# Softmax attention and an MLP on one core: q of two batches in pair layout, and the first MLP tiles placed ahead of the second attention product

## The chip, the cores and the metric

The kernel runs on one core of a Trainium2 chip. The metric is the device time of one execution in microseconds (us). The core has TensorE (PE) for matrix products, with a second row (PEld) for its weight loads, VectorE (DVE), ScalarE (ACT), GpSimd (POOL) and SyncE (SP), which here does nothing but issue DMAs. SBUF is the working memory with 128 partitions; PE writes its results into PSUM, from which DVE or ACT must move them (an "evacuation").

## The reference

Inputs are q, k and v with 8 batches, 8 heads, 576 tokens and head size 64, and two weight matrices.

```python
q_s = softmax(q, axis=-1)            # over the 64 values of a token
k_s = softmax(k, axis=2)             # over the 576 tokens
kv  = einsum('bhsd,bhse->bhde', k_s, v)
x   = einsum('bhsd,bhde->bhse', q_s, kv)   # then heads side by side: 4608 x 512
h   = x @ w_in                       # 512 -> 2048
out = gelu(h) @ w_out                # 2048 -> 512, float32
```

## The kernel before, in words

The 4608 tokens are worked in nine chunks of 512. Chunk b (0 to 7) holds the first 512 tokens of batch b; the ninth holds the remaining 64 of each batch. All matrix products are bf16.

**Attention of a batch.** q, k and v are loaded as float32 (`load_main` L83, `load_pair` L92). ACT takes the exponential of q (`exp_q` L127) and of k (`exp_k` L147) and writes bf16; v is cast to bf16 with a column of ones beside it (`cast_v` L156), so that one product gives both kv and the sum over tokens that normalises k. `kv_mm` (L188) forms kv for half of the head pairs: 36 matmuls on quarters of the PE array (64 x 64), for two pairs of heads and nine groups of 64 tokens. `kv_norm` (L204) divides on DVE and writes `kvc`. `norm_q` (L228) sums the exponentials of each token on DVE and multiplies by the reciprocal, on POOL or DVE. q must then stand with the head size along the partitions: for batches 0 and 1 `tp_mm` (L243) transposes on PE, eight full 128 x 128 blocks for each half, and `tp_evac` (L261) evacuates into `qT`; later batches use a transposing DMA (`xbar_step` L272). `x_mm` (L284) multiplies `qT` by `kvc`, and `x_evac` (L315) writes `xT`, one tile of 128 x 512 for each head pair.

**MLP of a chunk.** `h_phase` (L335) makes 16 tiles h of 128 x 512, each from four matmuls (dm = 0 to 3, one for each `xT` tile), and ACT applies gelu (L333). `y_phase` makes four tiles of 128 tokens x 512 from 16 matmuls each; they are evacuated to `y_sb` and stored (`y_out` L360).

**Order.** The program writes out the order of every engine by hand (`manual_schedule`); each engine runs its own instructions in that order and waits on semaphores. All loads but the first piece of k go through SP, in the order in which L478 to L499 name them: q, k, v of batch 0, w_in in five blocks, w_out, q and k of batch 1, part of w_out, v of batch 1, and then batch 2. Three tiny loads called `touch` (L485) and that first k piece (L101) go through ACT's queue. A DMA takes one of eight semaphores in turn, so that an issue may first wait until an earlier DMA has landed. PE warms up on zeros (`warm` L472) until data are there.

**Around the change, batch 0** (L506 to L538): exp of q in six instructions and of k in two; norm of q in two halves, POOL and DVE; `tp_mm(0,0)`; two v casts on ACT and two on POOL; `kv_mm(0,0)`, two separate norms; `tp_mm(0,1)`; `x_mm(0,0)`; the first w_in block is cast by ACT (dm = 0) and POOL; `kv_mm(0,1)`, one joint norm; `x_mm(0,1)` (L534); then `h_phase(0)`, whose first group is tiles 0 and 1.

**Batch 1** (L563 to L616) is prepared while PE runs the y tiles of chunk 0: after y step 11 PE does the 16 transposes (L581), after step 13 `kv_mm(1,0)`, after part of step 15 `x_mm(1,0)` and `kv_mm(1,1)`; and two h tiles of chunk 1 are half done ahead of `x_mm(1,1)`. The last four w_out rows (`cast_wo(3, ...)`) arrive and are cast in the same stretch.

Of the kernel before, what the change touches and what calls it, by code (L numbers as in the profile page):

```python
# [16 lines left out]
def kernel(  # L17
# [13 lines left out]

    nc = tc.nc
    B, H, S, D = q.shape
    NT, DM = out.shape
    DF = moe_w_in.shape[1]
    J = 4
# [3 lines left out]
    NDM = DM // 128  # L42
    NDF = DF // 128
    NS = S // 64
    VW = D + 2

    singles = ctx.enter_context(tc.tile_pool(name="singles", bufs=1))
# [35 lines left out]
    def load_main(b, name, t, parts=1):  # L83
# [5 lines left out]
        for i in range(parts):  # L89
            nc.sync.dma_start(out=f[:, i * n:(i + 1) * n, :], in_=src[:, i * n:(i + 1) * n, :])  # L90

    def load_pair(b, name, t, parts=1):  # L92
        f = f32in.tile([128, HP, NS * D], FP32, tag=name + "f")
        st[b][name + "f"] = f
        src = t[b].rearrange("h (p n) d -> (h p) (n d)", n=NS).rearrange("(x q) f -> q x f", q=128)
        n = HP // parts
        for i in range(parts):
            h0 = i * n
            if b == 0 and name == "k" and i == 0:

                nc.scalar.dma_start(out=f[:, 0, :], in_=src[:, 0, :])  # L101
                h0 = 1
            nc.sync.dma_start(out=f[:, h0:(i + 1) * n, :], in_=src[:, h0:(i + 1) * n, :])  # L103
# [20 lines left out]
                in_=q[b, :, M:S, :].rearrange("h p d -> p h d"),  # L124
            )

    def exp_q(b, parts=1):  # L127

        e = attn_sb.tile([128, J, H, D], BF16, tag="eq")
        st[b]["eq"] = e  # L130
        dst = e.rearrange("p j h d -> p h j d")
        src = st[b]["qf"]
        if b == B:
            src = src.rearrange("p j h d -> p h j d")
        else:
            src = src.rearrange("p h (j d) -> p h j d", j=J)
        if parts == 1:
            sets = [(slice(i, None, 4), slice(u, None, 4)) for i, u in ((0, 0), (1, 1), (2, 3), (3, 2))]
        else:
            sets = []  # L140
            for h in (0, 4):
                sets += [(slice(h + i, h + i + n), slice(h + u, h + u + n))
                         for i, u, n in ((0, 0, 2), (2, 3, 1), (3, 2, 1))]
        for i, u in sets:
            nc.scalar.activation(out=dst[:, i], in_=src[:, u], func=AF.Exp)  # L145

# [18 lines left out]
        for hp in range(HP):  # L165
            cast_v(b, hp)

    def kv_tiles(b):


        if b == 0:
            p = [psum_h.tile([128, 512], FP32, tag="h", name="kv")[:, 0:256] for i in range(2)]
            ps = psum_a.tile([128, 4, 256], FP32, tag="a2", name="kv")
            st[b]["kvall"] = ps[:, 0::2]
            p += [ps[:, 0, :], ps[:, 2, :]]
        else:
            ps = psum_a.tile([128, 4, 256], FP32, tag="a2", name="kv")
            st[b]["kvall"] = ps
            p = [ps[:, i, :] for i in place]
        st[b]["kv"] = p  # L180

    place = [1, 2, 0, 3]

# [4 lines left out]
    def kv_mm(b, half):  # L188


        if "kv" not in st[b]:
            kv_tiles(b)
        for n in range(NS):
            for i in range(2):
                for hh in range(2):
                    hp = 2 * half + i
                    pr = slice(hh * 64, hh * 64 + 64)
                    c = slice((hh ^ i) * 64, (hh ^ i) * 64 + 64)
                    nc.tensor.matmul(  # L199
                        st[b]["kv"][hp][c, 0:D + 1], ek[b % 2][pr, hp, n, :],  # L200
                        v_aug[b % 2][pr, hp, n, 0:D + 1], start=(n == 0), stop=(n == NS - 1),
                    )

    def kv_norm(b, half=None):  # L204

        ps = st[b]["kvall"]
        if half is None:
            parts = [(ps, kvc[b], 4)]
        elif b == 0 and half == 0:
            parts = [(st[b]["kv"][hp].unsqueeze(1), kvc[b][:, hp:hp + 1], 1) for hp in range(2)]  # L210
        elif b == 0:
            parts = [(ps, kvc[b][:, 2:4], 2)]
        else:
            parts = [(ps[:, 1:3] if half == 0 else ps[:, 0::3], kvc[b][:, 2 * half:2 * half + 2], 2)]
        for src, dst, m in parts:
            rec = small.tile([128, 4], FP32, tag="reck")
            nc.vector.reciprocal(rec[:, 0:m], src[:, :, D])
            nc.vector.tensor_tensor(  # L218
                out=dst, in0=src[:, :, 0:D],
                in1=rec[:, 0:m].unsqueeze(2).to_broadcast([128, m, D]), op=ALU.mult,  # L220
            )
# [18 lines left out]
            in1=recq.unsqueeze(3).to_broadcast([128, J, w, D]), op=ALU.mult,  # L240
        )

    def tp_mm(b, half):  # L243
        if half == 0:
            st[b]["qT"] = attn_sb.tile([128, J, HP, 128], BF16, tag="qT", name="qT")
        if b == 1 and half == 1:
            ps = psum_a.tile([128, 2, J, 2, 128], BF16, tag="a2", name="tp")[:, 0]
        else:
            pool, tag = (psum_h, "h") if half == 1 else (psum_a, "a")
            ps = pool.tile([128, J, 2, 128], BF16, tag=tag)  # L250
        st[b][f"tp{half}"] = ps
        for i in range(2):
            hp = 2 * half + i
            for j in range(J):
                nc.tensor.transpose(  # L255
                    ps[:, j, i, :],
                    st[b]["eq"][:, j, 2 * hp:2 * hp + 2, :].rearrange("p h d -> p (h d)"),
                    identity,
                )

    def tp_evac(b, half, eng="v"):  # L261
        o = st[b]["qT"][:, :, 2 * half:2 * half + 2, :]
        if eng == "v":
            nc.vector.tensor_copy(out=o, in_=st[b][f"tp{half}"])
        else:
            nc.scalar.copy(out=o, in_=st[b][f"tp{half}"])

    def tp_step(b, half):
        tp_mm(b, half)
        tp_evac(b, half)  # L270

    def xbar_step(b):  # L272
        st[b]["qT"] = attn_sb.tile([128, J, HP, 128], BF16, tag="qT", name="qT")
        nc.sync.dma_start_transpose(
# [9 lines left out]
    def x_mm(b, half):  # L284

        for bb in range(B if b == B else 1):
            for r in range(2):
                for i in range(2):
                    hp = 2 * half + i
                    pr = slice(r * 64, r * 64 + 64)  # L290
                    c = slice((r ^ i) * 64, (r ^ i) * 64 + 64)
                    ps = st[b][f"x{hp}"]
                    if b < B:
                        nc.tensor.matmul(  # L294
                            ps[c, :], kvc_of(b, hp)[pr], st[b]["qT"][pr, :, hp, :],
                            start=True, stop=True,
                        )
                    else:
                        nc.tensor.matmul(  # L299
                            ps[c, bb * R:(bb + 1) * R], kvc_of(bb, hp)[pr],  # L300
                            st[b]["qT"][pr, bb // 2, hp, bb % 2 * R:(bb % 2 + 1) * R],
                            start=True, stop=True,
                        )
# [56 lines left out]
    def y_out(c, ps, j, eng="v"):  # L360
# [2 lines left out]
            nc.vector.tensor_copy(out=y_sb, in_=ps)  # L363
        else:
            nc.scalar.copy(out=y_sb, in_=ps)
        if c < B:
            dst = out[c * S:c * S + M, :].rearrange("(p j) n -> p j n", j=J)[:, j, :]
            nc.sync.dma_start(out=dst, in_=y_sb)
        else:
# [63 lines left out]
    def cast_wi_dm(i, w, dm, eng):  # L433
# [2 lines left out]
        r = n // 128  # L436
        o = wi_bf[:, dm, wi_off[i]:wi_off[i] + n].rearrange("p (c m) -> p c m", c=r)
        w = w[:, dm, 0:n].rearrange("p (m c) -> p c m", c=r)
        if eng is nc.scalar:
            eng.copy(out=o, in_=w)  # L440
        else:
            eng.tensor_copy(out=o, in_=w)

    def load_wo(i):
        w = wst.tile([128, 4, DM], FP32, tag="w")
# [29 lines left out]
            nc.tensor.matmul(ps, z[:, 0:128], z, start=True, stop=True)  # L475


    load_main(0, "q", q, 2)  # L478
    load_pair(0, "k", k, 2)


# [5 lines left out]
    load_pair(0, "v", v, 4)  # L487
    wi = [load_wi(i) for i in range(5)]
    wo = [load_wo(i) for i in range(3)]
    load_main(1, "q", q, 2)  # L490
    load_pair(1, "k", k, 2)
    wo.append(load_wo(3))
    for hp in range(2):
# [10 lines left out]


    table(AF.Exp)  # L506
    exp_q(0, parts=2)
    exp_k(0, parts=2)
    norm_q(0, 0, 2)
    norm_q(0, 1, 2, nc.vector)  # L510
    tp_mm(0, 0)
    cast_v(0, 0, nc.scalar)
    cast_v(0, 1, nc.scalar)
    tp_evac(0, 0, "s")
    warm(1)
    cast_v(0, 2, nc.gpsimd)
    cast_v(0, 3, nc.gpsimd)
    x_tile(0, 0, psum_y, "y")
    x_tile(0, 1, psum_y, "y")
    kv_mm(0, 0)  # L520
    kv_norm(0, 0)
    tp_mm(0, 1)
    tp_evac(0, 1)
    x_tile(0, 2, psum_a, "a")
    x_mm(0, 0)
    x_evac(0, 0, "s")
    cast_wi_dm(0, wi[0], 0, nc.scalar)
    for dm in range(1, NDM):
        cast_wi_dm(0, wi[0], dm, nc.gpsimd)
    kv_mm(0, 1)  # L530
    kv_norm(0, 1)
    x_evac(0, 1)
    x_tile(0, 3, psum_h, "h")
    x_mm(0, 1)  # L534
    x_evac(0, 2, "s")
    x_evac(0, 3)
    cast_wi(1, wi[1], "p")
    table(AF.Gelu)  # L538

    def ybank():  # L540
        return psum_y.tile([128, M], FP32, tag="y", name="ps")
# [3 lines left out]
    def a2bank(i):  # L545
# [2 lines left out]
        return pair[0][:, i]  # L548

    h_phase(0, {  # L550
        0: [lambda: cast_wi(2, wi[2], "v")],
        2: [lambda: cast_wi(3, wi[3], "v")],
        6: [lambda: cast_wi(4, wi[4], "v")],
        9: [lambda: cast_wo(0, wo[0])],
        12: [lambda: cast_wo(1, wo[1])],
    }, groups={0: 2, 4: 4, 8: 4}, banks={
        3: ybank, 6: ybank, 8: ybank,
        9: lambda: psum_a.tile([128, M], FP32, tag="a", name="ps"),
        10: lambda: a2bank(0), 11: lambda: a2bank(1),
    })  # L560


    exp_q(1, parts=2)  # L563
    exp_k(1, parts=2)
    table(AF.Gelu)
    cast_wo(2, wo[2])
    yps = [psum_h.tile([128, DM], FP32, tag="h", name="ps") for j in range(2)]
    yps += [psum_y.tile([128, DM], FP32, tag="y", name="ps") for j in range(2)]
    norm_q(1, 0, 2)
    norm_q(1, 1, 2, nc.vector)  # L570
    cast_wo(3, wo[3], 0, 2)
    for hp in range(HP):
        cast_v(1, hp, nc.gpsimd)
# [4 lines left out]

    for t in range(12):
        y_part(t, range(J))  # L580
    tp_step(1, 0)  # L581
    tp_step(1, 1)
    load(3)
    cast_wo(3, wo[3], 2, 1, "s")
    cast_wo(3, wo[3], 3, 1, "s")
# [36 lines left out]
    h_phase(1, {12: [lambda: cast_v_all(2)]}, t1=4)  # L622


    exp_q(2, parts=2)
    exp_k(2)
    exp_k(3)
    exp_q(3)
# [73 lines left out]
```

The softmax here doesn't subtract the row's maximum and nothing guards it: scores larger than these inputs give would overflow.

## Time and profile before

| what | value |
|---|---|
| median of 3 runs | 279.58 us (279.49 to 279.82) |
| profiled execution, its own time | 279.74 us |
| its span, first to last instruction | 278.0 us |
| PE busy | 270.0 us (97%) |
| ACT, DVE, POOL busy | 158.0, 100.7, 32.8 us |
| DMA | 50.10 MB, mean 180 GB/s |
| first h matmul (L327) begins | 14.3 us |
| batch 0: last piece of q, of k, of v landed | 6.62, 8.96, 11.85 us |
| first w_in block landed | 13.26 us |
| batch 1: last piece of q, of k, of v landed | 33.65, 36.49, 41.94 us |
| full-tile matmul, start to start | 0.215 us |

A row of the profile names a line of the kernel, an engine, an operation and its tiles (out<-in), the number of instructions, their busy time and the idle time of the engine just before them with what ended it. The chain of waits follows the work that ended last back from the end, at each step to what released it. Times count from the start of the span. A matmul's own duration (380 ns) is longer than the step from one to the next, since matmuls are pipelined.

### The profile page before, as it was taken

Reading aid. Unit: us, or ns where it says so; the run is one execution under the profiler, and the core shown is the slowest. Engines: PE = TensorE matmul, PEld = TensorE weight load, DVE = VectorE, ACT = ScalarE, POOL = GpSimd, SP = SyncE. Lnnn points to the kernel's source line nnn. Section 1 sums busy time; section 2 is a strip of 40 time slices with the busy share of each in tenths; the row PEclk is TensorE's granted clock in tenths of the full one; section 3 lists DMA queues with packets and bytes.
Section 4 is the critical chain, followed back from the end, with each engine's and each line's share of the span. In section 5 each row is a group of like instructions: output and inputs, shape, how many; then the busy total and the mean of one; then the engine's idle time right before and its main releaser. Section 6 shows DMA issues by size and latency. Waiting matters only on the chain.

```text
span 278.0 us, 4534 instructions
## 1 busy us (share of the span) xinstructions
PE 270.0 (97%) x1891; PEld 126.5 (46%) x1919; DVE 100.7 (36%) x153; ACT 158.0 (57%) x247; POOL 32.8 (12%) x26
## 2 busy tenths in 40 slices
PE   7899999999999999999999999999999999999995
PEld 3444454444444444444444444444444444444443
DVE  2876574319743540093008400651015200130012
ACT  4867675789377816791569246943683363136400
POOL 1520051002020220014000500050005000000000
PEclk9999999999999999999999999999999999999999
DMA  7999999963993139702981199017502500220033
GB/s 253 398 386 429 397 402 407 398 257 103 287 348 61 66 79 295 283 38 86 267 329 40 42 247 383 38 51 190 115 0 75 151 2 0 75 78 0 0 78 77
DMA packets 44980, 50.10 MB, mean 180 GB/s; under 512 B 20384, under 2 KB 29856, under 8 KB 44704
## 3 DMA queue, kind: packets, MB, share of 16 engines
q1 hardware_dynamic: 44560, 49.39, 53.5%
q10 hardware_dynamic: 400, 0.43, 0.6%
q8 instruction: 15, 0.25, 0.3%
q14 instruction: 5, 0.04, 0.0%
HBM read 36.70 MB, written 9.44 MB: 166 GB/s over the span
## 4 chain that ended last, share of the span: by engine, by line
PE 94%; DMA 2%; issue 1%; ACT 1%; SPq 1%; DVE 0%
PE ps L327 44%; PE ps L355 43%; DMA f<-in_k_dram 2%; PE kv L199 2%; PE ps L294 2%; PE ps L380 1%; PE pair L327 1%; ACT ek L150 0%; ACT v_aug L160 0%; PE ps L255 0%; SPq L90 0%; PE ps L299 0%; SPq L103 0%; PE tp L255 0%; DVE kvc L218 0%
## 5 line engine op out<-in xcount | busy, mean ns | idle before, releaser
L327 PE MATMUL ps<-xT,wi_bf 128*128 128x512 bf16 x557 | 124.2, 380 | 0.5
L355 PE MATMUL ps<-wo_bf,g 128*128 128x512 bf16 x543 | 122.1, 380 | 1.6 <-issue 1.1
L333 ACT ACTIVATE g<-ps 128x512 bf16<-128x512 f32 x142 | 83.5, 598 | 66.8 <-PE ps L327 66.8
L327 PEld LDWEIGHTS <-wi_bf 128*128 128x128 bf16 x576 | 56.1, 98 | 68.0 <-issue 0.5
L355 PEld LDWEIGHTS <-g 128*128 128x128 bf16 x560 | 53.9, 98 | 64.3 <-issue 0.4
L363 DVE COPY y_sb<-ps 128x512 f32<-128x512 f32 x33 | 22.7, 687 | 81.7 <-PE ps L355 78.6
L238 POOL TENSOR_TENSOR e<-e,recq 128x2048 bf16<-128x2048 bf16 (+1 forms) x9 | 25.7, 2855 | 176.2 <-DVE recq L237 141.5
L162 DVE CAST v_aug<-f 128x576 bf16<-128x576 f32 x24 | 16.4, 746 | 47.5 <-DMA f<-in_v_dram 47.5
L236 DVE TENSOR_REDUCE qsum<-e 128x16 f32<-128x1024 bf16 (+1 forms) x13 | 21.1, 1621 | 14.4 <-ACT e L145 14.3
L320 ACT CAST xT<-ps 128x512 bf16<-128x512 f32 x18 | 9.9, 588 | 28.8 <-PE ps L294 18.8
L145 ACT ACTIVATE e<-f 128x512 bf16<-128x512 f32 (+1 forms) x42 | 20.5, 556 | 3.5 <-DMA f<-in_q_dram 3.5
L150 ACT ACTIVATE ek<-f 128x2304 bf16<-128x2304 f32 (+1 forms) x10 | 17.2, 1728 | 0.5 <-DMA f<-in_k_dram 0.4
L318 DVE CAST xT<-ps 128x512 bf16<-128x512 f32 x17 | 11.0, 686 | 17.0 <-PE ps L294 14.1
L79 ACT ACT_TABLE_LOAD x9 | 11.5, 1283 | 2.8 <-issue 2.6
L475 PE MATMUL ps<-zeros 128*128 128x512 f32 (+1 forms) x15 | 9.2, 773 | 1.5 <-DVE zeros L500 1.5
L145 ACT ACT_TABLE_LOAD x7 | 9.0, 1283 | 0.1
L431 DVE CAST wi_bf<-w 128x512 bf16<-128x512 f32 x12 | 7.3, 654 | 2.2 <-DMA w<-in_moe_w_in_dram 1.9
L199 PEld LDWEIGHTS <-ek 64*64 64x64 bf16 x576 | 6.6, 105 | 2.6 <-ACT wo_bf L470 0.4
L199 PE MATMUL kv<-v_aug,ek 64*64 64x65 bf16 x576 | 7.2, 194 | 0.2 <-ACT v_aug L160 0.2
L294 PE MATMUL ps<-qT,kvc 64*64 64x512 bf16 x62 | 5.7, 391 | 0.8 <-DVE kvc L218 0.6
L238 DVE TENSOR_TENSOR e<-e,recq 128x1024 bf16<-128x1024 bf16 x4 | 6.2, 1546 | 0.1
L475 PEld LDWEIGHTS ps<-zeros 128*128 128x128 f32 x14 | 3.5, 260 | 6.0 <-issue 4.5
(39 smaller groups left out, 49.9 us busy)
## 6 DMA issues: line engine op xcount, KB each, us to landing
out_dram<-y_sb SPq DMA_DIRECT2D x32, 256.0 KB, 2.4
f<-in_k_dram SPq DMA_DIRECT2D x6, 1152.0 KB, 9.7
f<-in_v_dram SPq DMA_DIRECT2D x6, 1152.0 KB, 11.7
f<-in_q_dram SPq DMA_DIRECT2D x6, 1024.0 KB, 7.2
w<-in_moe_w_in_dram SPq DMA_DIRECT2D x6, 512.0 KB, 8.7
f<-in_v_dram SPq DMA_DIRECT2D x8, 288.0 KB, 6.8
f<-in_q_dram SPq DMA_DIRECT2D x4, 512.0 KB, 12.5
w<-in_moe_w_out_dram SPq DMA_DIRECT2D x2, 1024.0 KB, 11.7
```

The source lines that it names most:

```text
L79: nc.scalar.activation(out=scr[:, 1:2], in_=scr[:, 0:1], func=func)
L145: nc.scalar.activation(out=dst[:, i], in_=src[:, u], func=AF.Exp)
L150: nc.scalar.activation(out=ek[b % 2][:, i:i + n], in_=st[b]["kf"][:, i:i + n].rearrange("p x (n d) -> p x n d", n=NS), func=AF.Exp,)
L162: eng.tensor_copy(out=o, in_=i)
L199: nc.tensor.matmul(st[b]["kv"][hp][c, 0:D + 1], ek[b % 2][pr, hp, n, :], v_aug[b % 2][pr, hp, n, 0:D + 1], start=(n == 0), stop=(n == NS - 1),
L236: nc.vector.reduce_sum(out=qsum, in_=eq[:, :, hs, :], axis=AX.X)
L238: eng.tensor_tensor(out=eq[:, :, hs, :], in0=eq[:, :, hs, :], in1=recq.unsqueeze(3).to_broadcast([128, J, w, D]), op=ALU.mult,)
L327: nc.tensor.matmul(ps, wi_bf[:, dm, t * 128:(t + 1) * 128], st[c]["xT"][:, dm, :], start=(dm == 0), stop=(dm == NDM - 1),)
L333: nc.scalar.activation(out=st[c]["g"][:, t, :], in_=ps, func=AF.Gelu)
L355: nc.tensor.matmul(ps, st[c]["g"][:, t, j * 128:(j + 1) * 128], wo_bf[:, t, :], start=(t == 0), stop=(t == NDF - 1),)
L363: nc.vector.tensor_copy(out=y_sb, in_=ps)
L475: nc.tensor.matmul(ps, z[:, 0:128], z, start=True, stop=True)
```

## The change

Two things are changed together.

**Order in batch 0.** Tiles 0 and 1 of h are begun (dm = 0 and 1) ahead of `x_mm(0,1)` and ended (dm = 2 and 3) after it. `kv_mm(0,0)` gets the two-bank PSUM tile and one joint norm; `kv_mm(0,1)` gets two banks of the h pool and two norms. ACT evacuates xT tiles 0, 1 and 3 and DVE tile 2 (before: ACT 0 and 2, DVE 1 and 3). All four casts of the first w_in block are POOL's.

**q of batches 0 and 1.** A head pair has one head in partitions 0 to 63 and the other in 64 to 127, with eight consecutive tokens of 64 values in each partition (before: four tokens of all eight heads in each of 128 partitions). So q comes in four DMAs of 64 partitions (pieces of 2 KB) in place of two of 128 partitions (pieces of 1 KB). Exp is two instructions in place of six. The transposes are quarters of the array, 32 for each half in place of eight full ones, and the evacuations are four of 128 x 512 in place of two of 128 x 1024. The tokens of an output tile then lie in two interleaved sets of 64 rows, so that each of the chunks' y tiles is stored with two DMAs of 64 partitions.

```diff
+    def load_qpair(b):
+        f = f32in.tile([128, HP, M], FP32, tag="qf", name="f")
+        st[b]["qf"] = f
+        src = q[b, :, 0:M, :].rearrange("(x q) (p n) d -> q p x (n d)", q=2, n=NQ)
+        for i in range(2):
+            for hh in range(2):
+                nc.sync.dma_start(
+                    out=f[hh * 64:hh * 64 + 64, 2 * i:2 * i + 2, :], in_=src[hh, :, 2 * i:2 * i + 2, :]
+                )
...
+    def exp_qpair(b):
+        e = attn_sb.tile([128, HP, NQ, D], BF16, tag="eq", name="e")
...
+    def norm_qpair(b, i, eng):
+        eq = st[b]["eq"][:, 2 * i:2 * i + 2].rearrange("p x n d -> p (x n) d")
...
+    def tpq_mm(b, half):
+        if half == 0:
+            st[b]["qT"] = attn_sb.tile([128, HP, NQ, 64], BF16, tag="qT", name="qT")
+            tp = [psum_a.tile([128, 2, NQ, 64], BF16, tag="a", name="tp")]
...
+        for n in range(NQ):
+            for i in range(2):
+                for hh in range(2):
+                    pr = slice(hh * 64, hh * 64 + 64)
+                    c = slice((hh ^ i) * 64, (hh ^ i) * 64 + 64)
+                    nc.tensor.transpose(
+                        st[b]["tp"][i][c, half, n, :], st[b]["eq"][pr, 2 * half + i, n, :],
+                        identity[pr, pr],
+                    )
...
+        if c < 2:
+            dst = out[c * S:c * S + M, :].rearrange("(p j i) n -> j i p n", j=J, i=2)
+            for i in range(2):
+                nc.sync.dma_start(out=dst[j, i], in_=y_sb[i * 64:i * 64 + 64, :])
...
-    load_main(0, "q", q, 2)
+    load_qpair(0)
...
-    load_main(1, "q", q, 2)
+    load_qpair(1)
...
-    exp_q(0, parts=2)
+    exp_qpair(0)
     exp_k(0, parts=2)
-    norm_q(0, 0, 2)
-    norm_q(0, 1, 2, nc.vector)
-    tp_mm(0, 0)
+    norm_qpair(0, 0, nc.gpsimd)
+    norm_qpair(0, 1, nc.vector)
+    tpq_mm(0, 0)
     cast_v(0, 0, nc.scalar)
     cast_v(0, 1, nc.scalar)
-    tp_evac(0, 0, "s")
+    tpq_evac(0, 0, "s")
+    tpq_evac(0, 1, "s")
...
     kv_mm(0, 0)
     kv_norm(0, 0)
-    tp_mm(0, 1)
-    tp_evac(0, 1)
-    x_tile(0, 2, psum_a, "a")
+    tpq_mm(0, 1)
+    tpq_evac(0, 2)
+    tpq_evac(0, 3)
     x_mm(0, 0)
     x_evac(0, 0, "s")
-    cast_wi_dm(0, wi[0], 0, nc.scalar)
-    for dm in range(1, NDM):
+    x_evac(0, 1, "s")
+    for dm in range(NDM):
         cast_wi_dm(0, wi[0], dm, nc.gpsimd)
     kv_mm(0, 1)
     kv_norm(0, 1)
-    x_evac(0, 1)
+    h_begin(0)
+    hps = [psum_h.tile([128, M], FP32, tag="h", name="ps"),
+           psum_a.tile([128, 2, M], FP32, tag="a2", name="ps")[:, 0]]
+    for dm in (0, 1):
+        for t in range(2):
+            h_mm(0, hps[t], t, (dm,))
     x_tile(0, 3, psum_h, "h")
     x_mm(0, 1)
-    x_evac(0, 2, "s")
-    x_evac(0, 3)
+    x_evac(0, 2)
+    x_evac(0, 3, "s")
     cast_wi(1, wi[1], "p")
     table(AF.Gelu)
+    for dm in (2, 3):
+        for t in range(2):
+            h_mm(0, hps[t], t, (dm,))
+    for t in range(2):
+        h_gelu(0, hps[t], t)
+    cast_wi(2, wi[2], "v")
...
-    exp_q(1, parts=2)
+    exp_qpair(1)
...
-    tp_step(1, 0)
-    tp_step(1, 1)
+    tpq_mm(1, 0)
+    tpq_evac(1, 0)
+    tpq_evac(1, 1)
+    tpq_mm(1, 1)
+    tpq_evac(1, 2)
+    tpq_evac(1, 3)
```

## The prediction

> **What bounds the kernel now.** I read the page's parts 1 and 2, then the chain of waits, then the DMA view.
>
> ```profile
> PE 270.0 (97%) x1891; PEld 126.5 (46%) x1919; DVE 100.7 (36%) x153; ACT 158.0 (57%) x247; POOL 32.8 (12%) x26
> ```
>
> TensorE is busy almost throughout, so time can only be won or lost where it starts late or stalls. The chain, in order of time (start, us, what), shows that start:
>
> ```profile
> 2.34 6.62 DMA f<-in_k_dram
> 8.98 1.16 ACT ek L150
> 10.15 1.15 ACT v_aug L160 x2
> 11.33 0.47 PE kv L199 x34
> 11.81 0.55 PE ps L255 x8
> 12.36 0.52 PE ps L294 x2
> 12.88 0.53 PE kv L199 x31
> 13.43 0.18 DVE rec L217
> 13.64 0.30 DVE kvc L218
> 13.98 0.41 PE ps L294 x4
> 14.39 0.75 PE ps L327 x3
> ```
>
> The reader should see a load as the first 9 us: the last part of k is queued behind all of q. The PE work before 10 us is warm-up. After it, PE waits once more, 13.4 to 13.98, for batch 0's second kv normalisation. From 14.3 us the MLP streams at 0.215 us a matmul, and 15.20 is where dm = 2 of tiles 0 and 1 begins.
>
> The stages next (length; busy time of PE, PEld, DVE, ACT, POOL; clock, DMA share, GB/s):
>
> ```profile
> 14.30:28.10 13.80, 13.70 (x66) 6.25 (x65) 9.43 (x15) 9.83 (x18) 1.36 (x3) 1.00 1.04 410
> 28.10:38.50 10.40, 10.35 (x48) 4.70 (x48) 7.31 (x8) 7.50 (x11) 1.90 (x1) 1.00 1.04 400
> 38.50:45.50 7.00, 6.80 (x116) 3.66 (x117) 4.29 (x10) 3.48 (x7) 2.70 (x4) 1.00 1.06 402
> ```
>
> The DMA engines are full up to 45.5 us. So a load that takes more engine time delays everything queued behind it, up to batch 1's v. How near that v is to being late stands in the timeline:
>
> ```profile
> 41.29 1.37 POOL L162 CAST v_aug<-f 128x576 bf16<-128x576 f32 x2 [1.34 <-DMA f<-in_v_dram]
> 43.27 0.51 PE L199 MATMUL kv<-v_aug,ek 64*64 64x65 bf16 x36
> ```
>
> POOL waits for v, ends the casts at 42.66, and PE uses them at 43.27: 0.6 us of slack.
>
> Last, the DMA view of two stretches: 268.2 to 271.5 us, where two stores of 64 partitions lie alone, and 11.5 to 13.5 us, with 1 KB packets into all 128 partitions (packets, MB, share of 16 engines).
>
> ```profile
> q1 hardware_dynamic: 160, 0.26, 34.1%
> out_dram<-y_sb SPq DMA_DIRECT2D x2, 128.0 KB, 2.2
> ```
> ```profile
> q1 hardware_dynamic: 772, 0.77, 108.9%
> ```
>
> First: 0.341 x 3.3 us x 16 / 128 data packets = 141 ns for a 2 KB packet (the packet records give a mean of 137, median 146; 32 of the 160 packets are semaphores). Second: 1.089 x 2 x 16 / 772 = 45 ns for 1 KB (records: 46). A 2 KB packet of a 128-partition load takes 84 in the records. A 64-partition transfer thus runs at some 60% of the full rate.
>
> [...] no load of 2 KB pieces into 64 partitions is in this trace. [...] The trace shows 36 quarter matmuls in 0.41 us (41.29 to 41.70).
>
> **The change, part by part.** Sums are made against the profiled execution: 279.74 us, of which 278.0 is span and 1.74 around it; the median of the runs is 0.16 lower.
>
> *q loads.* Two DMAs of 512 KB (1024 packets of 1 KB) become four of 256 KB (512 packets of 2 KB), each into 64 partitions. Before: 1024 x 46 / 16 = 2.9 us of full engines. After: 512 x 137 / 16 = 4.4. Ends: 512 x 84 / 16 = 2.7 if alternate halves overlapped, a gain of 0.25; 512 x 147 / 16 = 4.7 without any overlap. I take **+1.5 us per load**, as the stores are the nearest row. It happens twice (batches 0 and 1), with DMA full behind both.
>
> *What the two extra issues move.* An issue takes SP some 0.5 us. More important, eight DMAs may be outstanding, each on its own semaphore, and by the waits in the changed build SP's first k issue waits for the k part that ACT loads (landed 3.88), its second for the first q part, and the v issues behind it for the tiny touch loads (5.2, 6.5). So k is issued at about 3.9 instead of 1.8. A quiet store has its first packet 0.83 us after issue, so k is ready at 4.8, while q streams until about 2.3 + 0.8 + 4.4 = 7.5: hidden. If q were fast (until 5.8) it would still be hidden.
>
> *Exp and norm of q, batch 0.* One 128x1024 exp for three: about 1.05 us (128x1152 takes 1.16) for 1.24. ACT then waits for k anyway, so nothing. Both norms stay as they are.
>
> *Quarter transposes.* 32 for 8 in each half: at the kv pace, 32 x 0.41/36 = 0.36 us against 0.45 now[...]. From −0.1 to +0.45 each, four times, two of them on PE's path in batch 1. I take 0.
>
> *Evacuations.* ACT gets two of 128x512 (0.58 each by the xT row) for one of 1.00. They end at 1.16 after the v casts; kv_mm and its norm (0.5 + 0.5) cover nearly all: +0.05.
>
> *Batch 0 in sequence,* with +1.5 on each landing. v part 1: 10.46 to 11.96; k's last: 8.96 to 10.46. ACT: exp k to 11.62, casts to 12.9. kv_mm 12.9, kvc at 13.9 (one joint norm for two), x_mm 14.05, both evacuations now on ACT: xT0 15.1, xT1 15.7. The first w_in block lands 13.26 + 1.5 = 14.8; all four casts, one of which ACT did before, go to POOL at 0.37 each: 15.2, 15.55, 15.9, 16.3. So the h matmuls that now stand ahead of the second x run from 15.2 and 15.75 to 16.2. kv_norm 1 (two parts, 0.8 for 0.5) is ready at 15.5 and hidden. But x_mm 1 follows only at 16.2, and its evacuation (0.45 to its start, 0.7 long) has **nothing left to hide it**: dm = 2 begins at 17.4, where it was 15.2. So +2.2: 1.5 from the load, 0.7 from the order. The 0.6 us wait for kvc goes; the wait for the last two xT takes its place.
>
> *Batch 1.* By then the DMA queue is 2 x 1.5 = 3.0 late and PE 2.2. The norm of q's second half ends near 41.1 (landing 33.65 + 3.0, exp 1.05, sum 1.2, reciprocal 0.25, product 1.6 with gaps), behind it on DVE the w_out cast to 41.75; y tile 12, due at 39.40 + 2.2 = 41.6, waits 0.15. v's last: lands 41.94 + 3.0 = 44.95, cast to 45.7; kv_mm is then due at 43.27 + 2.35 = 45.6. So PE is late by 3.0 − 0.6 = **2.4**.
>
> *Stores.* Batches 0 and 1 store 64 rows at a time: 8 issues more on SP, 0.4 us each, and 128 packets a tile at 137 ns for 84, so 0.4 us more of the DMA engines for each of eight tiles. Behind them stand the loads of batches 3 and 4 and the transposing DMA of batches 2 and 3; those loads are used over 5 us after landing. Nothing.
>
> Sum: span 278.0 + 2.4 = 280.4; with 1.74 around it 282.1, on the median **282.0 us**.
>
> **Rivals.**
> - *The halves overlap* (the other side). Place: the q loads. If packets into alternate halves run at 84 ns, each load wins 0.25 and only the order's 0.7 is lost, with x evacuation partly covered: about +0.3, so 279.9, not slower by what can be told. It decides from a mean packet of 92 ns downwards (2.94 x 16 / 512). For it: four DMAs queue together, not two. Against: the stores. If besides the wait for xT is less than reckoned, this case ends faster, near 279.0.
> - *The queue runs dry.* v's issues wait for the touch loads; if these land past 9.5 us, v comes later than its place in the queue by 1 us or so: 283.0. Against: q's slow stream covers them.
> - *Quarters don't run in parallel,* so the change's array use is not what it says: 2 x 0.45 more on PE in batch 1: 282.9. Against: the kv row.
>
> **How the numbers follow.** Likeliest 0.74; halves overlap 0.14 (within 0.2%: 0.09, faster 0.05); queue dry 0.06; quarters serial 0.06. A measurement of this kernel can tell about 0.2%, 0.56 us. The likeliest's own range is 281.2 (load +1.1) to 283.0 (load +1.8); the whole range, 280.2 to 283.3, takes in the dear cases and half-overlapping loads and leaves out the overlap case. Faster 0.05, same 0.09, slower 0.86.
>
> **What would show it.** q packets of 2 KB near 137 ns, and k's last landing near 10.5 us; first kv_mm at 12.9; after x_mm 1 a PE gap of about 0.8 us for xT; batch 1's last v landing near 45; from there a constant shift. Wrong: q packets near 84, or a kv_mm start before 11.6.

## The result, and the profile after

The changed kernel takes 287.34 us (median of six; 284.92 to 287.75) against 279.53 before; the ratio of the means is 1.0267 (1.0232 to 1.0301). It is slower, as forecast, but by 7.8 us and not 2.4, and outside the range. The profiled execution is the fastest of the six (284.92 us); the five others lie between 287.18 and 287.75, and run 11 gives a profile of such a usual execution. All ratios in this document are of fast executions; the only slow one in all runs is one of run 10, at 285.22 us.

The page's busy row and the row of the granted TensorE clock, in 40 slices of 7.1 us:

```profile
PE 271.7 (96%) x1987; PEld 127.1 (45%) x2015; DVE 99.6 (35%) x155; ACT 157.1 (55%) x238; POOL 33.8 (12%) x27
PEclk9979999999999999999999999999999999999999
```

The "7" is what no step of the prediction had: for one stretch of 3.4 us, 14.29 to 17.71, TensorE had half its clock. Before, the clock never fell while TensorE worked (1.00 from 6.70 us to the end of the span). (The row shows 9 for the start too, but there the record of the clock has nothing: it begins at 6.70 us before and 7.46 after, and up to then the warm-up matmuls step 0.85 us, from then on 0.43. All stretches below are falls after that.)

The chain of waits up to 20 us (start, us, what):

```profile
2.21 5.45 DMA f<-in_q_dram
7.67 7.37 DMA w<-in_moe_w_in_dram
15.10 1.49 POOL wi_bf L466 x4
16.64 1.06 PE ps L350 x2
17.70 0.41 PE ps L318 x4
18.12 0.68 DVE xT L341
18.80 1.58 DVE wi_bf L458 x3
```

This is the predicted sequence: q's DMAs hold the queue, the first w_in block lands late (15.04), POOL casts it alone, the h matmuls run ahead of x (L318), and x's evacuation (xT) stands in the open. But it runs on to 18.8 (18.12 + 0.68; the last row is DVE's next cast) where 17.4 was foreseen. Of the DMA view, 32.5 to 35 us, q of batch 1:

```profile
DMA packets 362, 0.69 MB, mean 275 GB/s; under 512 B 38, under 2 KB 38, under 8 KB 362
q1 hardware_dynamic: 362, 0.69, 107.0%
```

1.07 x 2.5 us x 16 engines / 324 data packets = 132 ns for a packet of 2 KB in this stretch: near the 137 taken from the stores (over the whole load the packet records give a mean of 122). Batch 1 in the timeline, first before, then after:

```profile
38.51 0.61 PE L255 MATMUL ps<-identity,e 128*128 128x128 bf16 x8
38.95 0.61 PE L255 MATMUL tp<-identity,e 128*128 128x128 bf16 x8
```
```profile
42.25 0.45 PE L177 MATMUL tp<-identity,e 64*64 64x64 bf16 x32
43.22 0.77 PE L177 MATMUL tp<-identity,e 64*64 64x64 bf16 x32 [0.53 <-DVE qT L185]
43.98 1.37 POOL L218 CAST v_aug<-f 128x576 bf16<-128x576 f32 x2 [0.67 <-DMA f<-in_v_dram]
45.75 0.48 PE L251 MATMUL kv<-v_aug,ek 64*64 64x65 bf16 x36
```

The second half of the quarter transposes waits 0.53 us for DVE to evacuate the first half's first PSUM tile, and some 0.3 more for the second one, inside the row (0.77 us where the first half took 0.45): both halves share two PSUM tiles now, where each half of the full blocks had one of its own. The prediction had no such wait. v is cast at 45.35, and kv follows without a wait.

To compare runs, five marks on TensorE: Y0 and Y1, the first y matmul of chunks 0 and 1; H1 and H2, the first h matmul of chunks 1 and 2; Y8, the first y matmul of the last chunk. Before they stand at 28.15, 58.42, 44.16, 74.34 and 260.56 us. Shifts against that, in us, one profiled execution each, with the stretches of half clock after the warm-up and before the last matmul:

```
run                     Y0     H1     H2     Y8    half clock (us)
after                 +3.65  +4.53  +4.97  +4.96   14.3-17.7
1  order only         +0.53  +0.53  +0.53  +0.52   none
2  q only             +5.08  +6.16  +6.61  +6.60   14.9-21.8
3  after, warm 6      +2.22  +7.20  +7.73  +7.73   44.9-48.3
4  after, q 128       +0.44  +1.32  +1.80  +1.79   none
5  before, 4x64       +2.50  +7.45  +7.46  +7.45   11.6-15.0, 45.7-49.2
6  before, 4x128      +1.48  +1.48  +1.49  +1.48   none
7  q 128, edits       +0.38  +1.18  +1.18  +1.18   none
8  after, edits       +4.38  +4.95  +4.96  +4.95   11.5-18.4
9  4x64, batch 1      -0.31  +5.89  +5.90  +5.90   40.8-47.6
10 4x128, touch k     +4.66  +4.66  +4.67  +4.67   14.9-21.7
11 after again        +6.03  +6.91  +7.33  +7.32   12.9-23.1
12 best of q 128      -0.08  +0.37  +0.37  +0.37   none
13 4x128, no touch    +0.68  +1.23  +2.15  +2.13   none
14 before, 2x64       +6.65  +7.25  +7.26  +7.25   12.3-22.6
```

From H2 on every run keeps its shift: what moves TensorE happens before H2, in the first 75 to 82 us.

### The profile page after: what moved, and what is told of

Read it like the earlier page. It is cut to its first block, busy times and chain, and to the rows that moved or that the text cites. A ratio compares the mean times of both kernels' runs of the same rounds, so it can differ in the third digit from the quotient of the medians.

```text
span 283.1 us, 4742 instructions
## 1 busy us (share of the span) xinstructions
PE 271.7 (96%) x1987; PEld 127.1 (45%) x2015; DVE 99.6 (35%) x155; ACT 157.1 (55%) x238; POOL 33.8 (12%) x27
## 4 chain that ended last, share of the span: by engine, by line
PE 76%; DMA 14%; DVE 5%; ACT 2%; issue 1%; SPq 1%; POOL 1%; ACTq 0%
PE ps L350 36%; PE ps L378 35%; DMA f<-in_q_dram 6%; DMA out_dram<-y_sb 3%; DMA w<-in_moe_w_in_dram 3%; PE ps L318 2%; PE kv L251 1%; DMA qT<-e 1%; PE ps L407 1%; DVE qsum L288 1%; DVE qsum L155 1%; DVE wi_bf L458 1%; SPq L101 1%; DVE e L157 1%; ACT e L201 1%
## 5 line engine op out<-in xcount | busy, mean ns | idle before, releaser
L290 POOL TENSOR_TENSOR e<-e,recq 128x2048 bf16<-128x2048 bf16 (+1 forms) x7 | 21.9, 3129 | 152.5 <-DVE recq L289 124.9
L288 DVE TENSOR_REDUCE qsum<-e 128x32 f32<-128x2048 bf16 (+1 forms) x9 | 16.2, 1802 | 10.9 <-ACT e L201 10.9
L341 DVE CAST xT<-ps 128x512 bf16<-128x512 f32 x16 | 10.4, 686 | 18.1 <-PE ps L318 15.3
L201 ACT ACTIVATE e<-f 128x512 bf16<-128x512 f32 x28 | 15.3, 617 | 0.1
L155 DVE TENSOR_REDUCE qsum<-e 128x16 f32<-128x1024 bf16 x4 | 4.8, 1205 | 9.3 <-ACT e L144 9.3
L157 POOL TENSOR_TENSOR e<-e,recq 128x1024 bf16<-128x1024 bf16 x2 | 3.8, 1902 | 29.0 <-DVE recq L156 29.0
L458 DVE CAST wi_bf<-w 128x512 bf16<-128x512 f32 x12 | 6.6, 620 | 0.2
L492 DVE CAST wo_bf<-w 128x2048 bf16<-128x2048 f32 (+1 forms) x4 | 4.8, 1206 | 4.9 <-DMA w<-in_moe_w_out_dram 4.9
```

Of the source, the lines that this page charges most:

```text
L288: nc.vector.reduce_sum(out=qsum, in_=eq[:, :, hs, :], axis=AX.X)
L290: eng.tensor_tensor(out=eq[:, :, hs, :], in0=eq[:, :, hs, :], in1=recq.unsqueeze(3).to_broadcast([128, J, w, D]), op=ALU.mult,)
L341: nc.vector.tensor_copy(out=st[b]["xT"][:, hp, :], in_=ps)
```

## The experiments

**1 and 2: each part alone.** Run 1 has the new order with the old q; run 2 the new q with the old order.

```diff
# 1: after, with load_main / exp_q / norm_q / tp_mm / tp_evac of before for q
# 2: after, with the order, casts, PSUM tiles and evacuations of batch 0 of before
```

> The order alone: q of batches 0 and 1 is loaded, transposed and stored as in the kernel before; in batch 0 the first h matmuls stand ahead of the second x product, with the kv tiles, norms, evacuations and casts of the changed kernel. The theory that the order costs 0.7 us (the evacuation of the last two xT tiles has no cover left): 279.6 + 0.3 to 0.8 = 280.0 to 280.4, clock 1.00. The rival that the order is what gives TensorE its gaps and so halves its clock: a window at half clock, 281.5 or more.

> The q part alone (loads into 64 partitions, quarter transposes, stores of 64 rows, and exp of batch 2 in four instructions), in batch 0 with the order of the kernel before. The theory that the load is the cost and the clock only follows from gaps that the order makes: 279.6 + 1.8 (start) + 0.9 (batch 1) + 0.4 (batch 2) = 282.5 to 283, clock 1.00. The rival that the late load itself leaves TensorE too idle in one window, whatever the order: half clock appears here too, 284.5 to 287.5.

Measured: order alone 1.0025 (1.0015 to 1.0034), 280.3 us; q alone 1.0254 (1.0234 to 1.0273), 286.8 us. The order's timeline on TensorE:

```profile
13.57 1.04 PE L385 MATMUL ps<-xT,wi_bf 128*128 128x512 bf16 x3 [0.48 <-DVE kvc L276]
14.53 0.41 PE L353 MATMUL ps<-qT,kvc 64*64 64x512 bf16 x4
15.73 1.45 PE L385 MATMUL ps<-xT,wi_bf 128*128 128x512 bf16 x6 [0.79 <-POOL wi_bf L486]
```

h starts earlier (14.32 before), but x ends at 14.9 and dm = 2 begins only 0.8 us later, at 15.73 instead of 15.20: +0.53, where +0.7 was foreseen. The row names a cast of POOL for this wait; the last two xT evacuations end at the same moment, at 15.61 and 15.68. Nearly all of the loss is the q part, and run 2 loses its clock too, with the old order: its rival came true.

**3: does the clock make the rest?** More warm-up matmuls ahead of the first kv, so that TensorE isn't idle there.

```diff
-    warm(1)
+    warm(6)
     cast_v(0, 2, ...)
```

> The changed kernel with six instead of one warm-up matmul between the first transposes and kv_mm of batch 0, which fills the idle time of TensorE there. The theory that the half clock costs 1.4 us in the profiled execution and 4 in the usual one: clock 1.00 and 282.8 to 283.8. The rival that the clock matters little and the loads set the time: 286.5 to 287.5 as the changed kernel.

Measured: 1.0353 (1.0333 to 1.0373), 289.2 us: slower than the change itself. The expectation that the filler gains in total fell, but it splits the loss in two. At the start the clock did not fall; there dm = 2 began at 17.42, for the 17.4 foreseen, and Y0 is +2.22 us, for +2.2:

```profile
17.42 6.63 PE L350 MATMUL ps<-xT,wi_bf 128*128 128x512 bf16 x30 [0.79 <-POOL wi_bf L455]
```

The half clock moved into batch 1:

```profile
41.75 0.45 PE L177 MATMUL tp<-identity,e 64*64 64x64 bf16 x32 [0.86 <-POOL e L157]
44.23 0.77 PE L177 MATMUL tp<-identity,e 64*64 64x64 bf16 x32 [2.04 <-DVE qT L185]
45.34 3.15 PE L378 MATMUL ps<-wo_bf,g 128*128 128x512 bf16 x7 [0.33 <-issue]
48.42 0.48 PE L251 MATMUL kv<-v_aug,ek 64*64 64x65 bf16 x36
```

TensorE now comes to batch 1 only 2.2 us late, finds q not normalised (0.86), then waits 2.04 for the evacuation, which stands on DVE behind the w_out cast; then seven matmuls take 3.15 us, 0.45 each, twice the full-clock step. In this execution the last q of batch 1 landed at 38.01, later than in the changed kernel's first profile (36.75). There a late q of batch 1 is hidden because the start is later still.

**4 and 7: the same layout from 128 partitions.** Partition p of a head takes tokens 9p to 9p + 7, so that two heads of 64 partitions are one DMA of 128 with the same 2 KB pieces (token 9p + 8 goes to the ninth chunk). Run 7 adds y step 11 between the two transpose halves, evacuates the first half on ACT, and takes the exp of batch 2's q in six instructions again. The change had made them four (`exp_q(2)`), a part of it that neither its description nor the prediction has.

```diff
-        src = q[b, :, 0:M, :].rearrange("(x q) (p n) d -> q p x (n d)", ...)
-            for hh in range(2):
-                nc.sync.dma_start(out=f[hh*64:hh*64+64, 2*i:2*i+2, :], in_=src[hh, ...])
+        src = q[b].rearrange("h (p n) d -> (h p) (n d)", n=9).rearrange("(x q) f -> q x f", q=128)
+            nc.sync.dma_start(out=f[:, 2*i:2*i+2, :], in_=src[:, 2*i:2*i+2, 0:M])
```

> The changed kernel, but batches 0 and 1 keep tokens 9p to 9p+7 in partition p and leave tokens 9p+8 to the last chunk, so that a q load is two DMAs of all 128 partitions in pieces of 2 KB; all else is unchanged, stores too. The theory that 64 partitions make the load slow: v of batch 0 lands 0.2 us earlier than in the kernel before (10.2 to 10.5 us), no half clock, and 279.6 + 0.7 (order) + 0.4 (exp of batch 2) = 280.3 to 281.3. The rival that two more issues and their waits for semaphores delay the queue[...]: the same, as the issues go too; then the mean packet of q in the changed kernel tells them apart, and here 84 ns a packet is expected. The rival that neither is the cause: 285 to 287.5.

> The run with q loads of 128 partitions, with two edits more: in batch 1 one y step stands between the two halves of the transposes, and ACT evacuates the first half (so the second half no longer stands waiting for that evacuation, whose PSUM tiles it shares); and the exp of batch 2 is again six instructions, so that the first half's norm need not wait for the second. The theory that these two waits are the 0.9 us (batch 1) and 0.5 us (batch 2) that the stage times of that run show beyond the kernel before: 281.1 to 281.6, with the stages as long as before within 0.2 us. The rival that quarter transposes themselves are slower: batch 1 keeps 0.5 us or more, 282 or more.

Measured: run 4 1.0112 (1.0096 to 1.0127), 282.7 us, of which the marks show 1.8; its profile ends 4.6 us after the last matmul, for 3.4 before, which is most of the rest; run 7 1.0063 (1.0045 to 1.0081), 281.5 us. The DMA view of 3 to 9 us, first the changed kernel, then run 4:

```profile
DMA packets 969, 1.68 MB, mean 280 GB/s; under 512 B 184, under 2 KB 184, under 8 KB 969
```
```profile
DMA packets 1295, 2.42 MB, mean 404 GB/s; under 512 B 191, under 2 KB 191, under 8 KB 1295
```

With 128 partitions the queue is back at full rate (q packets 84 to 86 ns), k's last part lands at 8.65 and not 10.84, no stretch of half clock is left while TensorE works, and Y0 is +0.44. So the load carries the start's loss, the clock's share included. Run 4 also has two DMAs less for each q; runs 5, 6, 13 and 14 tell that from the 64 partitions. What stays, +0.88 from Y0 to H1 and +0.48 from H1 to H2, is not the load: it is the same +0.88 and about the same +0.44 as in the changed kernel. Run 7 takes the second away wholly (Y1 to H2 15.93 us as before, for 16.40); the first stayed at 0.80, where the expectation was 0.2 at most: ACT got to the evacuation only at 39.09, behind an ACT table load, and the second transposes still waited for it.

**5, 9 and 14: the slow load alone.** The kernel before, with q in halves of the partitions: run 5 in four DMAs in both batches, run 9 in batch 1 only, run 14 in two DMAs (no extra issue).

```diff
-            nc.sync.dma_start(out=f[:, i*n:(i+1)*n, :], in_=src[:, i*n:(i+1)*n, :])
+            for u in range(0, 128, 64):          # 14: all eight heads in each half
+                nc.sync.dma_start(out=f[u:u+64, i*n:(i+1)*n, :], in_=src[u:u+64, ...])
```

> The kernel before, with only the q loads of batches 0 and 1 cut into four DMAs of 64 partitions (pieces of 1 KB as before), layout and all else unchanged. The theory that loading half of the partitions is what costs: the DMA rate falls to 200 to 300 GB/s while q lands, v of batch 0 lands 1.5 to 2 us later, and with the idle time of TensorE a window at half clock: 283 to 287. The rival that the quarter transposes and their waits are the larger part: 280 to 282.

> The kernel before, with only batch 1's q loaded in four DMAs of 64 partitions; batch 0 is untouched. The theory that such a load slows the queue for 6 us (to 200 to 290 GB/s) and that v of batch 1 has 0.6 us of slack: start as before, y of chunk 0 to the next h 2 to 3 us longer, or 4 to 5 with a window at half clock: 281.7 to 284.7. The rival that batch 1 was late in the runs with both loads only because it inherited batch 0's delay: 279.6 to 280.5.

> The kernel before with q of batches 0 and 1 in two DMAs, each of 64 partitions and all eight heads, in place of two of 128 partitions and four heads; as many issues, k issued as early as before. The theory that 64 partitions slow the queue by themselves: the DMA rate is 200 to 300 GB/s while q lands, k's last part lands 1 us or more later than 8.96, and batch 1's v 2 us or more later than 41.9; 283 to 287. The rival that only the number of issues counts: landings within 0.4 us of the kernel before, and 279.6 to 281 (exp of q's first half must now wait for all of q).

Measured: run 5 1.0227 (1.0194 to 1.0260), run 9 1.0198 (1.0152 to 1.0244), run 14 1.0290 (1.0259 to 1.0321). Run 5, the kernel before with nothing but the load changed, loses 6.1 us, for the change's 7.8; less of it falls at the start (Y0 +2.50) and more in batch 1, where nothing hides the late q. Run 14 loses 7.8, but there each DMA brings all eight heads, so that the exp of q can't begin before all of q has landed (9.15 us); TensorE stands idle for 4.40 us before its first transposes, at 14.13. In run 14 the DMA view of 3 to 9 us has, where it had 386 GB/s before:

```profile
DMA packets 1360, 1.56 MB, mean 259 GB/s; under 512 B 143, under 2 KB 1119, under 8 KB 1360
```

k's last part lands at 11.21 in run 14, with two DMAs, and at 11.22 in run 5, with four: two suffice, so their number isn't the cause. Run 9 shows batch 1 without the start's delay as cover; its timeline, of ACT, POOL and TensorE:

```profile
35.00 1.28 ACT L147 ACT_TABLE_LOAD   x1 [6.37 <-DMA f<-in_q_dram]
39.23 1.90 POOL L240 TENSOR_TENSOR e<-e,recq 128x1024 bf16<-128x1024 bf16 x1 [23.75 <-DVE recq L239]
41.18 1.03 PE L257 MATMUL ps<-identity,e 128*128 128x128 bf16 x8 [2.82 <-POOL e L240]
43.33 3.58 PE L357 MATMUL ps<-wo_bf,g 128*128 128x512 bf16 x8
```

q comes late (its last part lands at 37.09, for 33.65 before), its exp and norm with it, TensorE idles 2.82 us, and then runs at half clock (eight transposes 1.03 us for 0.61, eight matmuls 3.58 for 1.89). One execution of run 9 kept the full clock: 283.27 us, against 285.66 to 286.46. By that one execution a slow q in batch 1 costs 3.6 us by its wait (283.27 − 279.72) and 2.4 to 3.2 more by the clock, if it isn't hidden. Runs 9 and 14 came out above their expected ranges (281.7 to 284.7, 283 to 287), by the clock in run 9.

**6, 10 and 13: the extra issues alone.** q in four DMAs of 128 partitions. In run 6 SP's k issues wait for semaphores (1.3 us), as in the changed kernel; run 10 adds a tiny early load on k (in place of that on w_out), in case untouched memory was slow; run 13 leaves the three tiny loads out, so that semaphores are free.

```diff
-    load_main(0, "q", q, 2)        # and batch 1
+    load_main(0, "q", q, 4)
# 10: the third touch reads k instead of w_out;  13: no touch
```

> The kernel before, with only the q loads of batches 0 and 1 cut into four DMAs of two heads each, over all 128 partitions: as many issues and the same waits for semaphores as in the changed kernel. The theory that the number of issues is hidden: 279.4 to 280.1. The rival that the issues and their semaphores delay k and v: 281 or more.

> The run with q in four DMAs over all partitions, with one edit: the third tiny early load reads 16 rows of k of batch 0 in place of w_out. In that run k and v packets of up to 1.4 us stood at 6.8 to 9 us, where the kernel before has none over 0.33. The theory that k's first accesses are slow when they come late and nothing has touched that memory before: with k touched those packets are gone, k's last part lands at 9.0 us in place of 10.4, and 279.6 to 280.4. The rival that the place of the issues in the queue does it: as that run, 281 to 284.5.

> The kernel before with q of batches 0 and 1 in four DMAs over all partitions, and without the three tiny early loads, so that eight DMAs suffice for q, k and the first v piece and k is issued without waiting for a semaphore. The theory that the wait for a semaphore (k issued at 4 us, behind which its packets come in with gaps) is the 1.4 us: k's last part lands at 9.0 to 9.3 in place of 10.4 to 10.7. The rival that the number of DMAs itself disturbs the queue: still 10.4 or later. What v and the weights lose without their early touch comes on top, after that.

Measured: 1.0105 (1.0051 to 1.0160), 1.0120 (1.0086 to 1.0154) and 1.0069 (1.0040 to 1.0097). SP's issues in run 6 and in run 13:

```profile
0.73 2.01 SPq L90 DMA_DIRECT2D f<-in_q_dram  x4
4.07 0.82 SPq L103 DMA_DIRECT2D f<-in_k_dram  x2
```
```profile
0.73 1.99 SPq L90 DMA_DIRECT2D f<-in_q_dram  x4
2.77 0.95 SPq L103 DMA_DIRECT2D f<-in_k_dram  x2
```

Issued at 4.07, k's last part lands at 10.44; at 2.77, at 9.63, between what the theory and the rival of run 13 had; before (1.79), at 8.96. In run 6, 17 packets of k and v (2304 bytes each) took over 300 ns after 6.5 us, up to 1449; in run 13 none did. Run 10 has them too (18), so untouched memory isn't the reason; what makes them long stays open. Run 13 also loses 0.9 us between Y1 and H2, which was not followed up. Behind a slow q this wait is hidden: run 5 has it and run 14 hasn't, and their k lands at 11.22 and 11.21.

Run 10 prices the clock. Its executions fall into two groups: four at 280.6 to 281.4 us (mean 281.0) with a mean clock of 0.998 or more, seven at 283.8 to 284.6 (mean 284.2) with 0.988, which is two stretches. The same program with two stretches of half clock takes 3.2 us more. The first group has no profile, so its loads may have landed earlier as well; run 6, profiled without a stretch, has k 0.29 us earlier than run 10 (10.44 for 10.73) and Y8 3.19 us earlier, which leaves some 2.9 for the clock.

**8 and 11: the changed kernel again.** Run 8 has run 7's two edits on it; run 11 is the change once more, for a second profile.

```diff
-    exp_q(2)
+    exp_q(2, parts=2)
...
-    tpq_evac(1, 0); tpq_evac(1, 1)
+    tpq_evac(1, 0, "s"); tpq_evac(1, 1, "s"); y_part(11, range(J))
```

> The changed kernel with those same two edits, q loads of 64 partitions kept. The theory that the loads make the start and the waits make much of batch 1's loss: the stage of batch 1 (y of chunk 0) takes 16.0 to 16.5 us where the changed kernel's took 16.9, and 284.5 to 286 in all. The rival that batch 1 simply waits for the late loads: the stage as long as in the changed kernel and 286.5 to 287.3.

> The changed kernel once more, for a second profiled execution, since the first was the fastest of six, with one window at half clock where the others have a mean clock that fits two or three. Theory: the usual execution also has a window at half clock in batch 1 (42 to 50 us), where TensorE waits for q and its transposes; the median stays at 287.3. Rival: it is the start that has more windows.

Measured: run 8 1.0236 (1.0182 to 1.0291), 285.4 us; run 11 1.0255 (1.0235 to 1.0275), 286.9 us. Run 8's Y0 to H1 is 16.58 us, for 16.89 in the changed kernel and 16.01 before: a part of that wait is gone. Its H1 to H2 is 30.19 us, for 30.62 in the changed kernel and 30.18 before. The wait behind this second one: first SP and TensorE of the changed kernel, then of run 8:

```profile
72.15 1.69 SPq L297 DMA_TRANSPOSE qT<-e  x1
75.94 0.63 PE L318 MATMUL ps<-qT,kvc 64*64 64x512 bf16 x8 [0.37 <-DMA qT<-e]
```
```profile
71.64 1.83 SPq L303 DMA_TRANSPOSE qT<-e  x1
75.93 0.63 PE L324 MATMUL ps<-qT,kvc 64*64 64x512 bf16 x8
```

The transposing DMA needs the exp and norm of q; with four coarse instructions instead of six it starts later, and x of batch 2 waits 0.4.

Run 11 is a usual execution of the change: three stretches of half clock, all at the start and none in batch 1, as the rival had it. TensorE there:

```profile
11.04 0.44 PE L177 MATMUL tp<-identity,e 64*64 64x64 bf16 x32 [1.05 <-POOL e L157]
11.41 0.39 PE L499 MATMUL ps<-zeros 128*128 128x512 bf16 x1
12.95 0.26 PE L251 MATMUL kv<-v_aug,ek 64*64 64x65 bf16 x2 [1.14 <-ACT v_aug L216]
13.52 0.70 PE L251 MATMUL kv<-v_aug,ek 64*64 64x65 bf16 x34 [0.31 <-ACT v_aug L216]
```

q and v are late, the warm-up has run out, and TensorE works for a moment and waits for another. The busy times of whole clock windows show what follows (from:to and length; busy time and instructions of PE, PEld, DVE, ACT, POOL; granted clock, DMA share, GB/s). First run 11:

```profile
9.46:12.87 3.41, 1.30 (x35) 0.53 (x34) 2.56 (x3) 2.58 (x4) 1.52 (x1) 1.00 1.04 401
12.87:16.28 3.41, 2.65 (x109) 2.13 (x109) 1.42 (x6) 2.29 (x6) 2.17 (x5) 0.50 1.08 396
16.28:19.70 3.42, 2.63 (x9) 0.67 (x9) 1.51 (x5) 1.32 (x3) 1.79 (x4) 0.50 1.05 400
```

then the changed kernel's profiled execution:

```profile
10.88:14.29 3.41, 1.79 (x84) 1.21 (x88) 2.17 (x5) 3.25 (x6) 1.51 (x3) 1.00 1.06 395
14.29:17.71 3.42, 3.04 (x77) 1.64 (x74) 1.45 (x6) 1.07 (x2) 2.78 (x7) 0.50 1.07 402
```

and the kernel before, at its weakest:

```profile
10.11:13.52 3.41, 3.05 (x94) 2.08 (x92) 2.25 (x7) 2.50 (x5) 1.54 (x3) 1.00 1.07 391
```

Here the windows of 3.41 us in which TensorE was busy for 1.30 (38%) and 1.79 (52%) were followed by one at half clock; the one with 3.05 (89%) wasn't. At half clock, the windows with 2.65 and 2.63 (78%, 77%) were followed by half clock again, the one with 3.04 (89%) by full clock.

**12: a version that loses nothing?** The 128-partition q in the old order, both first halves evacuated on DVE with y step 11 between, and batch 2's exp in six.

> q loads of 128 partitions in two DMAs (tokens 9p to 9p+7), order of batch 0 as in the kernel before, exp of batch 2 in six instructions, and the transposes' second halves not held up: the first halves are evacuated on DVE, and in batch 1 a y step stands between. Theory: every known cost is out; the load is some 0.3 us shorter and the start is as before or 0.2 earlier; stages of batch 1 and 2 as before: 279.3 to 279.9, no clear difference. Rival that quarter transposes or the stores of 64 rows cost by themselves: 280.3 or more.

Measured: 1.0038 (1.0025 to 1.0050), 280.7 us, clock full, Y0 −0.08. That is above the expected range and in the rival's, but the trace shows one more wait. H1 keeps +0.37; the second transposes take 0.77 us again:

```profile
39.06 0.77 PE L185 MATMUL tp<-identity,e 64*64 64x64 bf16 x32
```

Two of them start at 39.06, the others from 39.39 on, when DVE has evacuated the first half's second tile, behind a w_out cast. So the quarter transposes cost by this wait and not by their own pace. This version still doesn't gain over the kernel before, and the profile (280.22 us, the fastest of its six) doesn't show what the rest of its median is.

## Why the prediction was wrong

The step that failed first is one that the sum doesn't have. It takes TensorE at full clock in all its steps and gives the clock no term; but the clock fell to half at the start, for one to three stretches of 3.4 us, which cost 1.1 to 1.4 us in the first profile and 3.1 to 3.8 in the usual execution (worked out below). The second is the quarter transposes, which were put at 0 and measured +0.88. By the prediction's own steps:

- *q loads, +1.5 each:* that the load into 64 partitions makes all behind it late was right, the sizes only in sum. In the first profile batch 0's k and v came 1.9 us later and w_in 1.8; in run 11 these were 2.2 and 2.1, in run 3 1.5 and 1.4. Batch 1's q to v came 2.7 to 3.1 later, for 3.0, but that was luck, two errors that cancel: of batch 0's delay 0.8 us was left by then (third w_out block at 29.30, for 28.47), and the second load alone costs more than 1.5. In run 9, with batch 0 untouched, it makes q 3.4 us later, k 3.1 and v 3.0. The split was off as well: q's own packets took a mean of 117 ns in batch 0, less than the stores' 137, but the packets of k and v behind them 105 for 96.
- *Two extra issues hidden:* right behind a slow q (runs 5 and 14), though not free: alone they cost 1.5 us in run 6's profile, and its median is 2.8 us up, since two of its four executions lost the clock.
- *Order, +0.7:* +0.53 (run 1). *Batch 0, +2.2 together:* +2.22 where the clock did not fall (run 3, whose loads were 1.5 late as reckoned). Its signs came as foretold: the first kv at 12.63 (12.9), a gap of 0.80 us after the second x (0.8); under half clock dm = 2 then began at 18.85, not 17.4.
- *Quarter transposes, 0:* failed. At full clock they run nearly as fast as reckoned (32 in 0.45 us, for 0.36), but the second half waits for the first half's evacuation: +0.88 from Y0 to H1, in the changed kernel and in runs 4 and 11 alike.
- *Batch 1, v's slack 0.6 and a wait of 0.15 for q:* failed. Where TensorE came as early as reckoned (run 3) or on time (run 9), it was held by q's norm, in run 3 by the evacuation too, for 2.9 and 2.8 us, and not by v. In the changed kernel TensorE comes so late that this is hidden.
- *Not in the sum at all:* the exp of batch 2's q, +0.44, and the clock. The prediction had the clock of before as 1.00 in its stages and took that as given for the changed kernel.
- *Stores and loads of later batches, nothing:* right; H2 and Y8 shift alike.

For the usual execution (run 11) Y8 is +7.32: 2.2 at the start, 0.88 and 0.42 in batches 1 and 2, and 3.8 left over at the start, with its three stretches of half clock. That 3.8 is a difference (6.03 − 2.22) between two programs, and not all of it need be clock: run 11's first w_in block landed 0.7 us later than run 3's (15.39, 14.69). So the clock's share is 3.1 to 3.8; the 2.9 to 3.2 for two stretches in run 10 are of the same size. In the first profile, with one stretch: 2.2 + 1.4 + 0.88 + 0.44 = 4.9; its w_in landed 0.35 later than run 3's, so that up to 0.35 of the 1.4 may be load. Of run 11's excess over the predicted 2.4 us, 4.9, the start's rest is 3.8 and the two waits 1.3, less the 0.2 that batch 1 was to cost beyond the start. Why the load of one and the same program is quicker in one execution than in another stays open.

None of the rivals named this. "Halves overlap" was wrong by the packets, "queue dry" by the touch loads, which landed at 5.1 to 5.8 us and not past 9.5, "quarters serial" by 32 transposes in 0.45 us.

## What to carry to other kernels

Where a TensorE-bound kernel starts up behind a load, price a delay twice: the wait itself, and what the clock does if the wait thins out TensorE's work; here the windows of 3.4 us ahead of six falls were 23 to 53% busy. Lay loads over all 128 partitions even if two heads must share a DMA; the layout that looked the same with other tokens in it cost 1.1% instead of 2.7%. And a wait that is hidden behind an earlier delay comes back when that delay is mended: try each stage without the other's cover.

## What the runs showed of the hardware

**The clock fell after windows in which TensorE worked part of the time.** In the records of the kernel before and the changed kernel the stretches at one clock last 273.07, 6.83, 3.41 and 266.24 us: 80, 2, 1 and 78 windows of 3.413 us. The half-clock stretches of the table are one, two or three such windows, and their starts (14.3, 14.9, 44.9 us) show that the phase differs from run to run. In the changed kernel's first profile gaps of 0.3 to 0.6 us stood in the window ahead of the fall; ahead of the fall of run 11 gaps of 1.05 and 1.14, of run 3 0.86 and 2.04, of run 9 2.82, of run 14 4.40 (the last partly behind it). The table has ten falls; ahead of six of them the busy share of the window was 23% (run 14), 28% (run 9), 30% (run 3), 38% (run 11), 52% (the changed kernel) and 53% (run 2). Other windows kept the full clock: 61 and 80% (run 4), 66% (run 6), 82% (run 3), 89% (before), but also 44% (run 2) and 54% (run 6). So no single threshold in these shares tells them apart. The clock came back after windows with 89% (the changed kernel) and 90% (run 3), and not after 78 and 77% (run 11). Transposes, quarter tiles and full matmuls are counted alike in these shares; whether the hardware does so wasn't tried.

**Loads into half of the partitions slowed the queue beyond their own packets.** 1 KB packets took a mean of 73 and 75 ns in 64 partitions (run 14, batches 0 and 1) for 46 to 47 in 128 (before), and k's packets, which go to 128 partitions and are queued behind them, 107 and 118 for 98 and 93. Splitting the load into both halves didn't help, whether in four DMAs (run 5, k's last part at 11.22 us) or two (run 14, 11.21), for 8.96 before.
